# Moving the second MLP matrix to the end of a load stream, sharing nine slots, and writing the result in two halves

## The chip, the cores and the metric

The kernel runs on one core of a Trainium2 chip. The metric is the device time of one execution in microseconds (us). Before the change the median of the first three runs was 373.65 us. Ratios below are the mean time of one kernel's fast runs over the mean of the other kernel's fast runs of the same rounds on the same chip, so they are not quite the ratio of the medians quoted beside them.

Engines: PE multiplies matrices, PEld loads its stationary operand, DVE, ACT and POOL do elementwise work, and SP issues nearly all loads. A name such as SPq is an engine's instruction queue.

## The reference

A decode step for eight batch rows, in two branches that a gate mixes:

```python
x = A_x                                             # (8, 1, 576)
g = sigmoid((x * gate_w).sum(-1, keepdims=True))
q = x @ wq                                          # 32 heads of 128
k, v = the last 2048 rows of each of 16 K/V heads   # each serves 2 query heads
a = softmax(q k^T / sqrt(128)) v @ wo               # attention branch
b = gelu(layernorm(x) @ w1 + b1) @ w2 + b2          # MLP branch
return g * a + (1 - g) * b
```

All inputs are bf16. K and V are 134 MB of the 154 MB that are read; wq, wo, w1 and w2 are about 5 MB each. b2 has 576 elements.

## The kernel before

Every operation is recorded in a plan, a list scheduler on the host puts each engine's operations in an order, and that order is emitted. Each engine then executes its list in order and waits on semaphores. The scheduler has its own model of a load.

```python
class _Plan:
    DMA_BW = 428e3
    DMA_LAT = 1.8
    ...
    def schedule(self):
        ...
            if op.is_dma:
                eng_free[op.eng] = est + op.cost
                if op.nbytes < 65536:
                    op.t1 = est + 0.4 + self.DMA_LAT        # a small load: lands 2.2 us after its issue
                else:
                    start = max(est + 0.4, dma_free)        # a large one: behind those before it
                    dma_free = start + op.nbytes / self.DMA_BW
                    op.t1 = dma_free + self.DMA_LAT
```

The stream is made of units of 2 MB. A K unit is transposed by DVE and multiplied by PE, and four K units make the scores of one softmax group. A V unit is 64 small matmuls. Units are numbered from 0, so K31 and V31 are the last ones; the "last K pair" below is the two halves of K31. A unit's slot is free again when DVE (K) or PE (V) has used it. Before the change there are six slots, the output projection has 48 KB per partition of its own, W2 (`M` below) is loaded early, and V ends the stream:

```python
NSLOT = 6
stream = [("K", i) for i in range(4)] + [("M", i) for i in range(FC)]
stream += [("K", 4), ("W", 0), ("K", 5), ("W", 1), ("V", 0), ("W", 2), ("K", 6), ("W", 3)]
...                                              # then V and K in turn; V ends it
slot_free = [[o_qp], [o_qp], [o_qp], None, None, None]   # the first K waits for the query projection
```

Both branches add into one PSUM bank in `NJ` column groups that PE runs side by side. The bias is one such accumulation. Its load stands at the head, on ACT's queue:

```python
d_b2 = dma("act", lambda e: e.dma_start(b2_sb, B_b2.rearrange("(o d) -> o d", o=1)), "b", D * 2, name="d_b2", after=[d_b1])
...
o_m2 = [AccGroup("m2_b", [(ob[:, 0:8], b2_sb), (ob[:, 8:16], b2_sb)], db + [o_obl, o_obh], cost=0.6).op]
...
o_fin = add("dve", lambda e: e.tensor_copy(out_sb[0:104, :], ps[0:104, BK_ACC, 0:JN]), deps=acc_ops, name="fin", ...)
for j in range(NJ):                              # NJ = 4: two outputs on SP, two on ACT
    eng = "sp" if j % 2 == 0 else "act"
    fin.append(dma(eng, ... out2[:, JN * j:JN * j + JN], out_sb[32 * j:32 * j + 8, :] ...))
```

## Time and profile before

| what | number | where |
|---|---|---|
| time, span of the profiled run | 373.65 us, 372.1 us | runs, page |
| bytes read | 154.30 MB | DMA lines of the page |
| rate from 120 to 340 us | 430 GB/s at DMA share 1.01 | windows |
| a K load, issue to landing | 22.8 us | DMA issues of the page |
| first K issue | 24.71 us | timeline of SP |
| last landing to output issue | 368.04 to 369.76 us | timeline |

The table of forty slices on the page, lines for the DMA engines and for what they moved:

```profile
DMA  8999999999999999999999999999999999999992
GB/s 341 423 395 424 425 423 413 420 419 414 437 430 423 433 433 426 430 430 431 431 426 435 422 431 430 429 431 426 431 433 428 428 433 430 426 428 436 424 413 94
```

The DMA engines are busy from the first slice to the last, so only what keeps them idle or what stands before and after them can be saved. Three such places show. The first two are in the windows below. Columns are the stretch, its length, the busy time of each engine, the clock granted to PE, the share of the DMA engines that was busy, and the rate.

```profile
24.00:26.00 2.00, 1.48 (x30) 1.02 (x27) 0.42 (x1) 0.00 (x0) 0.00 (x0) 1.00 0.70 280
26.00:28.00 2.00, 0.27 (x3) 0.07 (x2) 0.00 (x0) 1.02 (x1) 0.53 (x3) 1.00 1.02 400
...
362.00:363.00 1.00, 0.70 (x26) 0.71 (x27) 0.00 (x0) 0.00 (x0) 0.00 (x0) 0.50 0.90 369
363.00:364.00 1.00, 1.00 (x44) 1.00 (x42) 0.00 (x0) 0.00 (x0) 0.00 (x0) 0.50 0.60 246
364.00:365.00 1.00, 0.80 (x31) 0.72 (x28) 0.00 (x0) 0.00 (x0) 0.00 (x0) 0.50 0.53 217
365.00:366.00 1.00, 0.38 (x15) 0.29 (x11) 0.00 (x0) 0.00 (x0) 0.00 (x0) 0.50 0.50 205
366.00:367.00 1.00, 0.59 (x16) 0.51 (x16) 0.00 (x0) 0.00 (x0) 0.00 (x0) 0.50 0.36 139
```

There is a small hole at 24 to 26 us, where the first K load waited for its slots, and a ramp at the end, where the share falls to about a half for some four microseconds. The packet records (the trace's list of every DMA packet with its start, duration and size) have 16 data packets in flight at 350 us and 8 at 365 us, so about half of the 16 DMA engines are done early. A window counts a whole packet where it starts. Spread over their durations, the packets put the hole at 26 to 28 us, with a share of 0.81, which is about 0.4 us of idle engines. The third place is the chain after the last landing, here from the timeline (start, duration, engine, line, operation):

```profile
368.05 0.59 PE L673 MATMUL ps<-arena 128*128 128x8 bf16 x16 [1.43 <-DMA arena<-in_A_v_cache_dram]
368.68 0.23 DVE L695 TENSOR_TENSOR arena<-ps,arena 128x16 bf16<-128x16 f32 x1 [13.64 <-PE ps L673]
368.96 0.41 PE L534 MATMUL ps<-arena 128*8 128x144 bf16 x8 [0.32 <-DVE arena L695]
369.42 0.31 DVE L729 CAST arena<-ps 104x144 bf16<-104x144 f32 x1 [0.52 <-PE ps L534]
369.76 0.75 SPq L733 DMA_DIRECT2D out_dram<-arena  x2
```

### The profile page before, as it was taken

How to read it: one execution, taken by the hardware profiler on the slowest of the kernel's cores; microseconds unless marked ns; L12 is line 12 of the kernel's file. 1: busy time of each engine (PE TensorE's matmuls, PEld its weight loads, DVE VectorE, ACT ScalarE, POOL GpSimd, SP SyncE). 2: the span in 40 equal slices, each digit the busy share in tenths (PEclk: the TensorE clock that was granted, in tenths of full speed). 3: DMA queues.
4: the chain of work that ended last, by engine and by line, in shares of the span. 5: the costliest groups of instructions: out<-in, count | busy, mean ns of one | idle time of the engine just before them, and what ended most of it. 6: DMA issues, size and time to landing. Idle time of an engine off the chain costs nothing.

```text
span 372.1 us, 7310 instructions
## 1 busy us (share of the span) xinstructions
PE 254.1 (68%) x3259; PEld 138.9 (37%) x3259; DVE 210.4 (57%) x253; ACT 28.3 (8%) x84; POOL 37.5 (10%) x163
## 2 busy tenths in 40 slices
PE   0169995661684987496749786877859774987554
PEld 0159432230341553243324443433415332543453
DVE  1414596934159645974468646954585448754600
ACT  1010001100002000200020001100020002000300
POOL 7003011010100110010100110011001010000000
PEclk9999999695865988788886868697659666788855
DMA  8999999999999999999999999999999999999992
GB/s 341 423 395 424 425 423 413 420 419 414 437 430 423 433 433 426 430 430 431 431 426 435 422 431 430 429 431 426 431 433 428 428 433 430 426 428 436 424 413 94
DMA packets 15097, 154.77 MB, mean 416 GB/s; under 512 B 1349, under 2 KB 5462, under 8 KB 6234
## 3 DMA queue, kind: packets, MB, share of 16 engines
q1 hardware_dynamic: 14992, 154.28, 97.9%
q8 instruction: 25, 0.41, 0.4%
q10 hardware_dynamic: 74, 0.03, 0.0%
q14 instruction: 6, 0.05, 0.0%
HBM read 154.30 MB, written 0.01 MB: 415 GB/s over the span
## 4 chain that ended last, share of the span: by engine, by line
DMA 50%; DVE 25%; PE 15%; SPq 8%; issue 1%; DVEq 0%
DMA arena<-in_A_k_cache_dram 37%; DVE arena L629 15%; PE ps L643 11%; DMA arena<-in_B_w_dram 7%; DMA arena<-in_A_v_cache_dram 6%; DVE arena L595 4%; DVE arena L576 4%; SPq L666 3%; SPq L719 2%; PE ps L491 2%; SPq L614 2%; DVE arena L585 1%; DVE arena L579 1%; PE ps L493 1%; PE ps L639 0%
## 5 line engine op out<-in xcount | busy, mean ns | idle before, releaser
L629 DVE STREAM_TRANSPOSE arena<-arena 128x2048 f32<-128x2048 f32 x64 | 145.6, 2298 | 85.8 <-DMA arena<-in_A_k_cache_dram 79.9
L643 PE MATMUL ps<-arena 128*128 128x512 bf16 x512 | 161.8, 476 | 39.0 <-DVE arena L629 39.0
L643 PEld LDWEIGHTS ps<-arena 128*128 128x128 bf16 x512 | 55.5, 115 | 133.5 <-issue 55.0
L673 PEld LDWEIGHTS ps<-arena 128*128 128x128 bf16 x2048 | 56.3, 97 | 13.7 <-DMA arena<-in_A_v_cache_dram 8.5
L673 PE MATMUL ps<-arena 128*128 128x8 bf16 x2048 | 56.7, 166 | 6.8 <-DMA arena<-in_A_v_cache_dram 6.8
L622 POOL COPY arena<-arena 32x32 bf16<-32x32 bf16 x128 | 26.0, 203 | 191.4 <-PE ps L643 175.5
L639 PE MATMUL ps<-arena 128*128 128x512 bf16 x32 | 14.9, 621 | 39.6 <-DVE arena L595 33.1
L576 DVE TENSOR_REDUCE arena<-ps 128x1 f32<-128x2048 f32 x8 | 18.3, 2292 | 27.1 <-PE ps L643 27.1
L590 ACT ACTIVATE arena<-ps,arena 128x512 bf16<-128x512 f32 x32 | 21.5, 685 | 111.2 <-DVE arena L585 111.2
L595 DVE STREAM_TRANSPOSE arena<-arena 128x512 bf16<-128x512 bf16 x32 | 19.9, 676 | 0.9 <-ACT arena L590 0.9
L639 PEld LDWEIGHTS ps<-arena 128*128 128x128 bf16 x32 | 3.5, 127 | 44.7 <-DVE arena L595 33.5
L689 ACT ACTIVATE arena<-ps 128x16 f32<-128x16 f32 x15 | 2.8, 184 | 182.2 <-PE ps L673 182.2
L695 POOL TENSOR_TENSOR arena<-arena 128x16 bf16<-128x16 f32 x15 | 4.0, 264 | 121.3 <-ACT arena L689 106.6
L534 PE MATMUL ps<-arena 128*8 128x144 bf16 (+1 forms) x280 | 8.4, 235 | 6.2 <-POOL arena L695 4.9
L491 PE MATMUL ps<-arena 128*128 128x8 bf16 x144 | 10.9, 201 | 1.7 <-DMA arena<-in_B_w_dram 1.7
L491 PEld LDWEIGHTS ps<-arena 128*128 128x128 bf16 x144 | 10.8, 157 | 2.2 <-DMA arena<-in_B_w_dram 2.2
L413 PE MATMUL ps<-arena 8*128 8x8 bf16 x8 | 0.5, 167 | 12.6 <-DVE arena L386 8.8
L534 PEld LDWEIGHTS ps<-arena 128*8 128x8 bf16 (+1 forms) x280 | 3.9, 84 | 11.3 <-POOL arena L695 5.7
L695 DVE TENSOR_TENSOR arena<-ps,arena 128x16 bf16<-128x16 f32 x1 | 0.2, 228 | 13.6 <-PE ps L673 13.6
L601 DVE RECIPROCAL arena<-ps 128x32 f32<-128x32 f32 x8 | 2.8, 353 | 7.9 <-PE ps L600 7.9
L493 PE MATMUL ps<-arena 128*128 128x8 bf16 x36 | 7.2, 201 | 0.0
L600 PEld LDWEIGHTS ps<-arena 128*128 128x128 f32 x16 | 4.2, 268 | 6.6 <-DVE arena L599 4.5
(78 smaller groups left out, 76.0 us busy)
## 6 DMA issues: line engine op xcount, KB each, us to landing
arena<-in_A_k_cache_dram SPq DMA_DIRECT2D x32, 2048.0 KB, 22.8
arena<-in_A_v_cache_dram SPq DMA_DIRECT2D x31, 2048.0 KB, 24.0
arena<-in_B_w_dram SPq DMA_DIRECT2D x4, 1296.0 KB, 16.1
arena<-in_B_w_dram SPq DMA_DIRECT2D x1, 4608.0 KB, 24.4
arena<-in_A_wo_dram SPq DMA_DIRECT2D x4, 1152.0 KB, 17.6
arena<-in_A_wq_dram SPq DMA_DIRECT2D x1, 4096.0 KB, 12.8
arena<-in_A_v_cache_dram SPq DMA_DIRECT2D x4, 512.0 KB, 21.9
arena<-in_B_w_dram SPq DMA_DIRECT2D x1, 576.0 KB, 25.6
```

Of the source, the lines that this page charges most:

```text
L491: ins = e.matmul(out_, lhsT, yT[:, kt, :], start=(kt == 0), stop=False)
L493: ins = e.matmul(out_, lhsT, yT[:, 4 + c // 2, :], start=False, stop=True)
L534: ins = e.matmul(ps[32 * j:32 * j + 8, BK_ACC, 0:JN], lhsT, rhs[:, JN * j:JN * j + JN], start=False, stop=True, skip_group_check=True, til ...
L576: mx = add("dve", lambda e: e.tensor_reduce(out=k(MX), in_=ps[:, 0:4, :].rearrange("p a n -> p (a n)"), axis=AXL.X, op=ALU.max), deps=[qk_ ...
L590: return e.activation(out=Pm[:, 512 * c:512 * c + 512], in_=ps[:, c, :], func=ACTF.Exp, bias=k(NB), scale=SCALE, accum_out=k(SUM + c))
L595: pts.append(add("dve", (lambda c=c: lambda e: e.transpose(PT[:, g % 2, 16 * c:16 * c + 16, :].rearrange("p r m -> p (r m)"), Pm[:, 512 * ...
L622: return e.tensor_copy(dst, src)
L629: tr = add("dve", (lambda h=h, kb=kb: lambda e: e.transpose(bass.AP(arena_f, offset=foffs("KT") + kb * 2048, ap=[[AST // 2, 128], [1, 2048]]),
L639: mm = e.matmul(ps[:, rc, :], maskL, maskR, start=True, stop=False)
L643: mm = e.matmul(ps[:, rc, :], qbd[:, ub, 2 * h + ee, :], rhs, start=False, stop=(q == 3 and h == 1 and ee == 1))
L666: d = dma("sp", (lambda pp=pp, w=w: lambda e: e.dma_start(slot(s)[:, pp * w:(pp + 1) * w], src[:, :, pp * w:(pp + 1) * w]))(), ("t%d" % pp ...
L673: mm = e.matmul(ps[:, BK_OS[item % 2], 8 * (q % 2):8 * (q % 2) + 8], slot(s)[:, r * 128:(r + 1) * 128], PT[:, g % 2, r, 8 * q:8 * q + 8], ...
```

## The change

Its intent is to shorten that last chain and to keep the stream fed. The projection weights no longer have memory of their own; they go through the slots, of which there are now nine. W2 ends the stream, because one W2 slice needs two matmuls before the result is complete, where V needs its products, the scaling and the projection. The result is accumulated in two column groups of 288 instead of four of 144, and evacuated by DVE and ACT at once, each with one write of its half. Two smaller moves come along: the small part of wq is loaded first, and b2 is broadcast to eight partitions and loaded on SP's queue just before W2.

```diff
-    NSLOT = 6
+    NSLOT = 9
-    NJ = 4
+    NJ = 2
-        req("wo", Hq * WOP, BF, 512)
...
-        d_b2 = dma("act", lambda e: e.dma_start(b2_sb, B_b2.rearrange("(o d) -> o d", o=1)), "b", D * 2, name="d_b2", after=[d_b1])
...
-        stream = [("K", i) for i in range(4)] + [("M", i) for i in range(FC)]
-        stream += [("K", 4), ("W", 0), ("K", 5), ("W", 1), ("V", 0), ("W", 2), ("K", 6), ("W", 3)]
+        stream = [("K", i) for i in range(5)]
...                      # K and V in turn; one W chunk after every eighth V
+        stream += [("B", 0)] + [("M", i) for i in range(FC)]
-        slot_free = [[o_qp], [o_qp], [o_qp], None, None, None]
+        slot_free = [[o_qp]] * 3 + [[o_hp]] * 3 + [[]] * 3
-            return (0, 1, 2, 0)[n] if n < 4 else (n - 3) % NSLOT
+            return (n + 6) % NSLOT
...
+        def bias(i):
+            d = dma("sp", lambda e: e.dma_start(b2_sb, B_b2.partition_broadcast(8)), "b2", 8 * D * 2, name="d_b2", after=last_dma[-1:])
+            last_dma.append(d)
+            o_m2.append(AccGroup("m2_b", [(ob[:, 0:8], b2_sb), (ob[:, 8:16], b2_sb)], [d, o_obl, o_obh], cost=0.6).op)
...                      # m2_chunk takes a slot; its last chunk is loaded in parts of 4, 3 and 2 slices
-        o_fin = add("dve", lambda e: e.tensor_copy(out_sb[0:104, :], ps[0:104, BK_ACC, 0:JN]), deps=acc_ops, name="fin", cost=0.3, prio=9)
+        for j, (eng, ev) in enumerate((("sp", "dve"), ("act", "act"))):
+            ...          # each engine evacuates one half of 288 columns, each queue writes one
```

More of the change, by code (lines that the diff above doesn't have):

```diff
@@ L183, in build_kernel @@
     NG = Hkv // HG
-    NSLOT = 6
+    NSLOT = 9
     SE = 4 * W
-    LEAD = 7
     FC, FJ = 4, 9
@@ L189, in build_kernel @@
     FCW = 128 * FJ
-    W2P = 5376
     WOP = 768
-    NJ = 4
+    NJ = 2
+    WO_CH = 8
     JN = D // NJ
@@ L245, in build_kernel @@
         req("o32", 2 * 16, F32)
-        req("oT", 2 * 16, BF)
+        req("oT", Hkv * 16, BF)
         req("out_sb", JN, BF)
@@ L294, in build_kernel @@
         b1T = view("b1T")
-        b2_sb = view("b2", 1)
+        b2_sb = view("b2", 8)
         u_sb, uh_sb, v1_sb, v2_sb = view("u"), view("uh"), view("v1"), view("v2")
         hT = view("hT").rearrange("p (t b) -> p t b", b=8)
-        ob = view("ob", 1)
-        ot32 = view("ot32", 1)
+        ob = view("ob", 8)
+        ot32 = view("ot32", 8)
         gb = view("gb")
@@ L305, in build_kernel @@
         o32 = view("o32").rearrange("p (u m) -> p u m", u=2)
-        oT = view("oT").rearrange("p (u h b) -> p u h b", u=2, h=2)
+        oT = view("oT").rearrange("p (u h b) -> p u h b", u=Hkv, h=2)
         out_sb = view("out_sb")
@@ L309, in build_kernel @@
         Pm = view("P")
-        wo_sb = view("wo").rearrange("p (t c) -> p t c", t=Hq)
         RAW = view("RAW")
@@ L325, in build_kernel @@
         w1_r = RAW[:, W1O + 4 * F:W1O + 4 * F + F // 2]
-        w2_sb = RAW[:, 3 * SE:3 * SE + FC * W2P].rearrange("p (c k) -> p c k", c=FC)
         def col(i, parts=128):
@@ L340, in build_kernel @@
         eng_sems = {e: es.enter_context(nc.semaphore("sem_" + e)) for e in ENGS}
-        dma_keys = ["x", "b", "wq", "w1", "wo", "out", "outb"] + ["w2_%d" % i for i in range(FC)] + ["s%d" % i for i in range(NSLOT)] + ["t%d" % i for i in range(4)]
+        dma_keys = ["x", "b", "b2", "wq", "w1", "out", "outb"] + ["s%d" % i for i in range(NSLOT)] + ["t%d" % i for i in range(4)]
         dma_sems = {k: es.enter_context(nc.semaphore("dma_" + k)) for k in dma_keys}
@@ L372, in build_kernel @@
         d_b1 = dma("act", lambda e: e.dma_start(b1c, B_b1.rearrange("(c f) -> c f", c=FC)), "b", F * 2, name="d_b1", after=[d_gw])
-        d_b2 = dma("act", lambda e: e.dma_start(b2_sb, B_b2.rearrange("(o d) -> o d", o=1)), "b", D * 2, name="d_b2", after=[d_b1])
         dx = [d_x, d_gw]
-        db = [d_b1, d_b2]
-        d_wqm = dma("sp", lambda e: e.dma_start(wq_m.rearrange("p t c -> p (t c)"), A_wq[0:512, :].rearrange("(p t) c -> p (t c)", t=4)), "wq", 512 * 8192, name="d_wqm")
-        d_wqr = dma("sp", lambda e: e.dma_start(wq_r, A_wq[512:576, :].rearrange("k (s c) -> (k s) c", s=2)), "wq", 64 * 8192, name="d_wqr", after=[d_wqm])
+        db = [d_b1]
+        d_wqr = dma("sp", lambda e: e.dma_start(wq_r, A_wq[512:576, :].rearrange("k (s c) -> (k s) c", s=2)), "wq", 64 * 8192, name="d_wqr")
+        d_wqm = dma("sp", lambda e: e.dma_start(wq_m.rearrange("p t c -> p (t c)"), A_wq[0:512, :].rearrange("(p t) c -> p (t c)", t=4)), "wq", 512 * 8192, name="d_wqm", after=[d_wqr])
         dwq = [d_wqm, d_wqr]
-        d_w1m = dma("sp", lambda e: e.dma_start(w1_m.rearrange("p t c -> p (t c)"), B_w1[0:512, :].rearrange("(p t) c -> p (t c)", t=4)), "w1", 512 * F * 2, name="d_w1m", after=[d_wqr])
+        d_w1m = dma("sp", lambda e: e.dma_start(w1_m.rearrange("p t c -> p (t c)"), B_w1[0:512, :].rearrange("(p t) c -> p (t c)", t=4)), "w1", 512 * F * 2, name="d_w1m", after=[d_wqm])
         d_w1r = dma("sp", lambda e: e.dma_start(w1_r, B_w1[512:576, :].rearrange("k (s c) -> (k s) c", s=2)), "w1", 64 * F * 2, name="d_w1r", after=[d_w1m])
@@ L441, in build_kernel @@
         o_gb = add("dve", lambda e: e.tensor_copy(gb, ps[:, BK_X, 384:400]), deps=[o_gp], name="gb_ev", cost=0.15)
-        o_obh = add("dve", lambda e: e.tensor_copy(ob[:, 0:8], gb[0:1, 8:16]), deps=[o_gb], name="ob_hi", cost=0.12)
+        o_obh = add("dve", lambda e: e.tensor_copy(ob[:, 0:8], dg[:, 8:16]), deps=[o_dgb], name="ob_hi", cost=0.12)
         o_ob32 = add("dve", lambda e: e.tensor_copy(ot32, ob[:, 0:8]), deps=[o_obh], name="ob_32", cost=0.12)
-        o_obl = add("dve", lambda e: e.tensor_tensor(out=ob[:, 8:16], in0=gb[0:1, 8:16], in1=ot32, op=ALU.subtract), deps=[o_ob32], name="ob_lo", cost=0.12)
+        o_obl = add("dve", lambda e: e.tensor_tensor(out=ob[:, 8:16], in0=dg[:, 8:16], in1=ot32, op=ALU.subtract), deps=[o_ob32], name="ob_lo", cost=0.12)
         o_i32 = []
@@ L541, in build_kernel @@
         NUQ = 4 * NG
-        stream = [("K", i) for i in range(4)] + [("M", i) for i in range(FC)]
-        stream += [("K", 4), ("W", 0), ("K", 5), ("W", 1), ("V", 0), ("W", 2), ("K", 6), ("W", 3)]
-        ki, vi = 7, 1
+        stream = [("K", i) for i in range(5)]
+        ki, vi = 5, 0
         while ki < NUQ or vi < NUQ:
-            if vi < NUQ:
-                stream.append(("V", vi)); vi += 1
             if ki < NUQ:
-                stream.append(("K", ki)); ki += 1
-        WO_CH = 8
-        d_woc = []
+                stream.append(("K", ki))
+                ki += 1
+            if ki >= 6:
+                stream.append(("V", vi))
+                if (vi + 1) % (NUQ // (Hq // WO_CH)) == 0:
+                    stream.append(("W", vi // (NUQ // (Hq // WO_CH))))
+                vi += 1
+        stream += [("B", 0)] + [("M", i) for i in range(FC)]
         last_dma = [d_w1r]
-        slot_free = [[o_qp], [o_qp], [o_qp], None, None, None]
+        slot_free = [[o_qp]] * 3 + [[o_hp]] * 3 + [[]] * 3
         n_slot = [0]
@@ L658, in v_unit, with pv_fn @@
             item = 2 * g + q // 2
-            final = (i == NUQ - 1)
-            src = src_of(A_v_cache, g, q)
-            parts = 4 if final else 1
-            prev = None
-            for pp in range(parts):
-                nr = 64 // parts
-                w = nr * 128
-                d = dma("sp", (lambda pp=pp, w=w: lambda e: e.dma_start(slot(s)[:, pp * w:(pp + 1) * w], src[:, :, pp * w:(pp + 1) * w]))(),
-                        ("t%d" % pp) if final else ("s%d" % s), 4 * W * Dh * 2 // parts, deps=slot_free[s] if pp == 0 else [], name="dv%d_%d" % (i, pp), after=last_dma[-1:])
-                last_dma.append(d)
-                def pv_fn(e, pp=pp, nr=nr):
-                    mm = None
-                    for r in range(pp * nr, (pp + 1) * nr):
-                        mm = e.matmul(ps[:, BK_OS[item % 2], 8 * (q % 2):8 * (q % 2) + 8], slot(s)[:, r * 128:(r + 1) * 128], PT[:, g % 2, r, 8 * q:8 * q + 8],
-                                      start=(q % 2 == 0 and r == 0), stop=(r == 63), skip_group_check=True)
-                    return mm
-                deps = [d] + pt_done[g]
-                if q % 2 == 0:
-                    deps += [o_item_ev[item - 2]] if item >= 2 else [o_qT, o_u]
-                prev = add("pe", pv_fn, deps=deps, name="pv%d_%d" % (i, pp), cost=2.2 / parts, after=[prev] + pv_hist[-1:])
+            d = dma("sp", lambda e: e.dma_start(slot(s), src_of(A_v_cache, g, q)), "s%d" % s, 4 * W * Dh * 2, deps=slot_free[s], name="dv%d" % i, after=last_dma[-1:])
+            last_dma.append(d)
+            def pv_fn(e):
+                mm = None
+                for r in range(64):
+                    mm = e.matmul(ps[:, BK_OS[item % 2], 8 * (q % 2):8 * (q % 2) + 8], slot(s)[:, r * 128:(r + 1) * 128], PT[:, g % 2, r, 8 * q:8 * q + 8],
+                                  start=(q % 2 == 0 and r == 0), stop=(r == 63), skip_group_check=True)
+                return mm
+            deps = [d] + pt_done[g]
+            if q % 2 == 0:
+                deps += [o_item_ev[item - 2]] if item >= 2 else [o_qT, o_u]
+            prev = add("pe", pv_fn, deps=deps, name="pv%d" % i, cost=2.2, after=pv_hist[-1:])
             pv_hist.append(prev)
@@ L686, in v_unit @@
                 hl = q // 2
-                pj = [proj_ops[item - 2]] if item >= 2 else []
                 if item < Hkv - 1:
@@ L690, in v_unit @@
                     o_item_ev[item] = ev
-                    eng, src_, deps = "pool", o32[:, item % 2, :], [ev, rg_done[g]] + pj
+                    eng, src_, deps = "pool", o32[:, item % 2, :], [ev, rg_done[g]]
                 else:
-                    eng, src_, deps = "dve", ps[:, bk, 0:16], [prev, rg_done[g]] + pj
+                    eng, src_, deps = "dve", ps[:, bk, 0:16], [prev, rg_done[g]]
                 def om_fn(e):
-                    return e.tensor_tensor(out=oT[:, item % 2, :, :].rearrange("p h b -> p b h"), in0=src_.rearrange("p (b h) -> p b h", h=2),
+                    return e.tensor_tensor(out=oT[:, item, :, :].rearrange("p h b -> p b h"), in0=src_.rearrange("p (b h) -> p b h", h=2),
@@ L696, in om_fn @@
                                            in1=rg[:, g % 2, 16 * hl:16 * hl + 16].rearrange("p (b h) -> p b h", h=2), op=ALU.mult)
                 oT_done[item] = add(eng, om_fn, deps=deps, name="oT%d" % item, cost=0.25, prio=9)
-                mms = [(oT[:, item % 2, h, :], wo_sb[:, 2 * item + h, 0:D]) for h in range(2)]
-                proj_ops[item] = AccGroup("proj%d" % item, mms, [oT_done[item]] + d_woc, cost=0.6, after=[g_.op for g_ in acc_groups[-1:]], prio=2).op
-        o_m2 = [AccGroup("m2_b", [(ob[:, 0:8], b2_sb), (ob[:, 8:16], b2_sb)], db + [o_obl, o_obh], cost=0.6).op]
@@ L703, in m2_chunk, with wo_chunk @@
-        def m2_chunk(ci):
-            d = dma("sp", lambda e: e.dma_start(w2_sb[:, ci, 0:FJ * D], B_w2[FCW * ci:FCW * ci + FCW, :].rearrange("(p j) n -> p (j n)", j=FJ)),
-                    "w2_%d" % ci, FCW * D * 2, deps=[o_hp], name="d_w2_%d" % ci, after=last_dma[-1:])
-            last_dma.append(d)
-            mms = [(hT[:, FJ * ci + j, :], w2_sb[:, ci, j * D:(j + 1) * D]) for j in range(FJ)]
-            o = AccGroup("m2_%d" % ci, mms, [o_hT, d], cost=2.5, after=o_m2[-1:]).op
-            o_m2.append(o)
-            for s in range(3, 6):
-                slot_free[s] = [o]
+        def wo_chunk(i):
+            s = take_slot()
+            h0 = WO_CH * i
+            dst = slot(s)[:, 0:WO_CH * WOP].rearrange("p (t c) -> p t c", t=WO_CH)
+            d = dma("sp", lambda e: e.dma_start(dst[:, :, 0:D], A_wo[128 * h0:128 * (h0 + WO_CH), :].rearrange("(t p) c -> p t c", p=128)),
+                    "s%d" % s, WO_CH * 128 * D * 2, deps=slot_free[s], name="d_wo%d" % i, after=last_dma[-1:])
+            last_dma.append(d)
+            ops = []
+            for item in range(h0 // 2, (h0 + WO_CH) // 2):
+                mms = [(oT[:, item, h, :], dst[:, 2 * item + h - h0, 0:D]) for h in range(2)]
+                ops.append(AccGroup("proj%d" % item, mms, [oT_done[item], d], cost=0.5).op)
+            slot_free[s] = ops
@@ new lines, in build_kernel @@
+        o_m2 = []
+        def bias(i):
+            d = dma("sp", lambda e: e.dma_start(b2_sb, B_b2.partition_broadcast(8)), "b2", 8 * D * 2, name="d_b2", after=last_dma[-1:])
+            last_dma.append(d)
+            o_m2.append(AccGroup("m2_b", [(ob[:, 0:8], b2_sb), (ob[:, 8:16], b2_sb)], [d, o_obl, o_obh], cost=0.6).op)
+        def m2_chunk(ci):
+            s = take_slot()
+            dst = slot(s)[:, 0:FJ * D]
+            src = B_w2[FCW * ci:FCW * ci + FCW, :].rearrange("(p j) n -> p (j n)", j=FJ)
+            cuts = [0, 4, 7, 9] if ci == FC - 1 else [0, FJ]
+            ops = []
+            for n, (j0, j1) in enumerate(zip(cuts, cuts[1:])):
+                d = dma("sp", (lambda j0=j0, j1=j1: lambda e: e.dma_start(dst[:, j0 * D:j1 * D], src[:, j0 * D:j1 * D]))(),
+                        ("t%d" % n) if ci == FC - 1 else ("s%d" % s), 128 * (j1 - j0) * D * 2, deps=slot_free[s] if n == 0 else [], name="d_w2_%d_%d" % (ci, n), after=last_dma[-1:])
+                last_dma.append(d)
+                mms = [(hT[:, FJ * ci + j, :], dst[:, j * D:(j + 1) * D]) for j in range(j0, j1)]
+                ops.append(AccGroup("m2_%d_%d" % (ci, n), mms, [o_hT, d], cost=0.25 * (j1 - j0), after=o_m2[-1:]).op)
+                o_m2.append(ops[-1])
+            slot_free[s] = ops
@@ L713, in build_kernel @@
         pv_hist = []
         for kind, i in stream:
-            if kind == "M":
-                m2_chunk(i)
-            elif kind == "W":
-                h0 = WO_CH * i
-                d = dma("sp", (lambda h0=h0: lambda e: e.dma_start(wo_sb[:, h0:h0 + WO_CH, 0:D], A_wo[128 * h0:128 * (h0 + WO_CH), :].rearrange("(t p) c -> p t c", p=128)))(),
-                        "wo", WO_CH * 128 * D * 2, name="d_wo%d" % i, after=last_dma[-1:])
-                last_dma.append(d)
-                d_woc.append(d)
-            elif kind == "K":
-                k_unit(i)
-            else:
-                v_unit(i)
+            {"K": k_unit, "V": v_unit, "W": wo_chunk, "M": m2_chunk, "B": bias}[kind](i)
@@ L728, in build_kernel, with ev_fn @@
         acc_ops = [g_.op for g_ in acc_groups]
-        o_fin = add("dve", lambda e: e.tensor_copy(out_sb[0:104, :], ps[0:104, BK_ACC, 0:JN]), deps=acc_ops, name="fin", cost=0.3, prio=9)
         fin = []
-        for j in range(NJ):
-            eng = "sp" if j % 2 == 0 else "act"
-            fin.append(dma(eng, (lambda j=j: lambda e: e.dma_start(out2[:, JN * j:JN * j + JN], out_sb[32 * j:32 * j + 8, :]))(), "out" if j % 2 == 0 else "outb", 8 * JN * 2, deps=[o_fin], name="d_out%d" % j, after=last_dma[-1:]))
+        for j, (eng, ev) in enumerate((("sp", "dve"), ("act", "act"))):
+            def ev_fn(e, j=j, ev=ev):
+                dst, src = out_sb[32 * j:32 * j + 8, :], ps[32 * j:32 * j + 8, BK_ACC, 0:JN]
+                if ev == "dve":
+                    return e.tensor_copy(dst, src)
+                return e.activation(out=dst, in_=src, func=ACTF.Copy)
+            o_fin = add(ev, ev_fn, deps=acc_ops, name="fin%d" % j, cost=0.4, prio=9)
+            fin.append(dma(eng, (lambda j=j: lambda e: e.dma_start(out2[:, JN * j:JN * j + JN], out_sb[32 * j:32 * j + 8, :]))(), "out" if j == 0 else "outb", 8 * JN * 2, deps=[o_fin], name="d_out%d" % j, after=last_dma[-1:]))
```

## The prediction

> What bounds it now. The kernel is a stream of loads. By the page's DMA lines it reads 154.30 MB; the table of forty slices shows DMA digit 9 almost throughout, and ten-microsecond windows between 120 and 340 us hold 424 to 436 GB/s at a DMA share of 1.00 to 1.02. The Trainium skill ("DMA: Bandwidth & Descriptors", "Where 436 GB/s comes from") puts the port ceiling at 435 GB/s and also says HBM loads bind at about 358; this trace agrees with the first and not the second. So the middle has 1% at most left, and SP's waits for slots there (157 us for the transposes, 90 for the V products, by the table of waits) are not lost time: loads take 23 us from issue to landing, so almost five are queued while SP waits. At 429 GB/s the bytes need 359.7 of the 372.1 us. The other 12 us are the start, the small-packet stretch, and the end.
>
> The change removes no bytes (b2 now goes to eight partitions, 8 KB more). Costed:
>
> 1. Early hole. SP issues the first K load at 24.71 us, after the query projection frees its slots; windows show 280 GB/s at 24 to 26 us (share 0.70), 400 at 26 to 28. By the packet records the engines lose about 0.4 us there, and the next stretch runs at 393 to 410 GB/s. With slots 6 to 8 free from the start, K is issued at about 3 us. Gain 0.4 to 1.0 us.
>
> 2. Output projection. Its 4096 packets of 1152 B take 51 ns each against 614 ns for 16 KB, about 2 us more in all than their bytes need (60 to 90 us: 409 to 414 GB/s). Only their place moves. SP was held up to 6.9 us at issues behind them; nine slots keep enough queued. Zero.
>
> 3. Ramp at the end. From 362.5 us half of the DMA engines have finished and the rest go on to 366.9: windows of 1 us fall from 369 to 246, 217, 205, 139, 0 GB/s. That costs 2.1 us. It is a spread between engines that builds up over the stream; the change does not address it. Zero, plus or minus 1.
>
> 4. Chain after the last landing (368.04 us by the timeline). Before: 16 products 0.60, DVE 0.24, projection 0.41, DVE 0.31, with waits 1.72 us to the output issue at 369.76; then two issues a queue, 0.75 us. After: two hT slices by two column halves, four matmuls of 288 columns, at the half clock seen there (0.50) about 0.6 us; then halves of 288 columns on DVE and ACT in parallel, about 0.45 (144 columns took 0.31; ACT's 512 took 0.68); one issue a queue, 0.37. Saves 0.5 and 0.4: 0.9 us.
>
> All of 1 and 4 lies on the critical path. The larger PE time of the accumulations (8.4 us becomes perhaps 12) does not: PE is busy 68% and waits. The last K now lands about 12 us earlier before the end (W2's bytes), so V products and projections finish under the W2 loads.
>
> Sum: 0.6 + 0.9 and a little = 1.6 us. Predicted 372.0 us, 80% range 370.2 to 373.5. Chances: faster by over 2%: 0.02; within 2%: 0.97; slower: 0.01.
>
> Right if: no dip at 24 to 28 us and first K issue near 3 us; middle rate unchanged at 429; landing to output issue near 1.2 us, one output issue per queue. Step 2 is wrong if the DMA share falls under 1.00 in the middle behind the 1152 B packets.
>
> What would make it wrong: the spread between engines growing or vanishing; the scheduler placing a projection so that PE stalls on a late load and slots come free late; W2's short last packets slower than V's.

## The result and the profile after

The kernel became slower: 386.15 us (384.64 to 387.64, 4 runs) against 373.6 us, ratio 1.0337 with a 95% interval of 1.0291 to 1.0383. The prediction was 372.0 us with a range of 370.2 to 373.5, so it was wrong, in size and in direction.

The same two lines of the page, of the kernel after (its span is 385.9 us, so a slice is 9.6 us):

```profile
DMA  8999999999999999999999999999999999999430
GB/s 343 451 401 426 431 429 427 433 428 428 431 426 433 419 428 433 426 433 431 425 431 416 430 427 430 428 433 430 433 428 417 430 430 428 433 422 390 166 155 1
```

Up to about 356 us the stream is as full as before. After that the DMA engines run dry and then stand idle for a slice. The group table of the page names a wait that the kernel before did not have, in the line of the accumulations (after the bars: busy time, mean ns, idle time just before them and what ended it):

```profile
L529 PE MATMUL ps<-arena 128*8 128x288 bf16 (+1 forms) x140 | 11.5, 326 | 32.4 <-DMA arena<-in_B_b_dram 32.4
```

PE stood 32.4 us, all of it in one piece, for a load of a bias. The timeline shows where. SP's and PE's lines of it:

```profile
316.86 0.53 SPq L704 DMA_DIRECT2D arena<-in_B_b_dram  x1
319.84 1.74 PE L662 MATMUL ps<-arena 128*128 128x8 bf16 x64
321.61 43.49 SPq L715 DMA_DIRECT2D arena<-in_B_w_dram  x6
353.94 0.64 PE L529 MATMUL ps<-arena 8*8 8x288 bf16 x4 [32.36 <-DMA arena<-in_B_b_dram]
354.51 6.08 PE L640 MATMUL ps<-arena 128*128 128x512 bf16 x16
360.44 3.34 PE L662 MATMUL ps<-arena 128*128 128x8 bf16 x128
368.67 0.64 PE L597 MATMUL ps<-arena 128*128 128x32 f32 x2 [4.89 <-DVE arena L596]
369.12 7.00 PE L662 MATMUL ps<-arena 128*128 128x8 bf16 x256
376.05 7.43 PE L529 MATMUL ps<-arena 128*8 128x288 bf16 x88
383.62 0.45 DVE L733 CAST arena<-ps 8x288 bf16<-8x288 f32 x1 [7.24 <-PE ps L529]
384.10 0.32 SPq L736 DMA_DIRECT2D out_dram<-arena  x1
```

The chain of waits has the same load as its longest piece:

```profile
316.86 37.03 DMA arena<-in_B_b_dram
```

The four bias matmuls (8x288) were reached at 321.6 us. Their load, 9 KB, had been issued at 316.86 us and was there 37.0 us later. By the packet records 14.7 MB of loads issued before it were still to be moved at that moment, which is 34 us at 430 GB/s (an estimate). Behind them in PE's list stood everything that was left: the last K pair's products, the last softmax, six V units, the projections and W2. When the bias was in, that chain took another 30 us to the output issue, and the loads had gone dry meanwhile, because slots come free only when PE has used them. This is SP's table of waits between 361 and 363 us:

```profile
SPq L715 <- PE ps L662: 14.0, 1, 14.0
```

SP could issue the third W2 chunk only at 362.2 us, after V products that were late. The windows show both sides, an idle PE under a full stream, and then an idle stream under a busy PE:

```profile
330.00:340.00 10.00, 0.00 (x0) 0.00 (x0) 0.00 (x0) 0.00 (x0) 0.00 (x0) 0.50 1.00 429
340.00:350.00 10.00, 0.00 (x0) 0.00 (x0) 0.00 (x0) 0.00 (x0) 0.00 (x0) 0.50 1.01 420
350.00:356.00 6.00, 2.06 (x8) 0.65 (x9) 0.00 (x0) 0.00 (x0) 0.00 (x0) 0.50 0.97 397
356.00:364.00 8.00, 7.78 (x141) 4.78 (x139) 3.10 (x8) 0.00 (x0) 0.00 (x0) 0.79 0.30 102
```

Why do the bias matmuls stand there? The scheduler's plan answers it. These are the planned times (start and end in its own model), beside which the chip's times are 353.9 us for the landing and 353.94 us for the matmuls:

```
SP:  d_wo3 313.0-350.2   d_b2 313.4-315.6   d_w2_0_0 317.3-353.3
PE:  pv25 315.0-317.2   m2_b 317.2-317.8   qk31_0 320.5-322.5   qk31_1 322.8-324.8   pv26 324.8-327.0
```

The load before b2 was planned to land at 350.2 us and the one behind it at 353.3 us, but b2 itself at 315.6 us, because it is smaller than 64 KB and such loads are modelled as landing 2.2 us after their issue. That shortcut did no harm while the small loads stood at the head on ACT's queue. The Trainium skill says how both queues really behave. "DMA: Bandwidth & Descriptors", section "Queues, rings and completion order", has SP and ACT each own one ring on each of the 16 DMA engines, with descriptors consumed in ring order. So a small load on SP's queue comes behind the megabytes issued before it on that queue. "TensorE: Matmul & The Clock Gate", section "Step-by-step: what each phase is for", says that matmuls stay in program order and that only weight loads are pulled ahead. This trace agrees with both: 37.0 us for 9 KB, and 32.4 us in which no matmul passed the waiting one.

### The profile page after: what moved, and what is told of

It is laid out like the page before. It is cut to its first block, busy times and chain, and to the rows that moved or that the text cites. A ratio compares the mean times of both kernels' runs of the same rounds, so it can differ in the third digit from the quotient of the medians.

```text
span 385.9 us, 7069 instructions
## 1 busy us (share of the span) xinstructions
PE 248.2 (64%) x3117; PEld 138.3 (36%) x3117; DVE 210.4 (55%) x253; ACT 28.6 (7%) x85; POOL 37.8 (10%) x163
## 4 chain that ended last, share of the span: by engine, by line
DMA 62%; PE 22%; DVE 14%; issue 1%; SPq 1%; ACT 0%; DVEq 0%; ACTq 0%
DMA arena<-in_A_k_cache_dram 46%; PE ps L640 12%; DMA arena<-in_B_b_dram 10%; DVE arena L626 9%; DMA arena<-in_B_w_dram 7%; PE ps L662 3%; DVE arena L573 3%; PE ps L486 2%; PE ps L529 2%; PE ps L636 1%; DVE arena L592 1%; DVE arena L576 1%; PE ps L488 1%; DVE arena L582 0%; SPq L656 0%
## 5 line engine op out<-in xcount | busy, mean ns | idle before, releaser
L640 PE MATMUL ps<-arena 128*128 128x512 bf16 x512 | 153.9, 458 | 35.0 <-DVE arena L626 35.0
L640 PEld LDWEIGHTS ps<-arena 128*128 128x128 bf16 x512 | 53.7, 111 | 125.0 <-issue 45.7
L662 PEld LDWEIGHTS ps<-arena 128*128 128x128 bf16 x2048 | 55.9, 97 | 11.5 <-DMA arena<-in_A_v_cache_dram 6.8
L662 PE MATMUL ps<-arena 128*128 128x8 bf16 x2048 | 55.8, 166 | 5.0 <-DMA arena<-in_A_v_cache_dram 5.0
L636 PE MATMUL ps<-arena 128*128 128x512 bf16 x32 | 14.9, 620 | 37.8 <-DVE arena L592 29.3
L529 PE MATMUL ps<-arena 128*8 128x288 bf16 (+1 forms) x140 | 11.5, 326 | 32.4 <-DMA arena<-in_B_b_dram 32.4
L529 PEld LDWEIGHTS ps<-arena 128*8 128x8 bf16 (+1 forms) x140 | 6.5, 96 | 37.0 <-DMA arena<-in_B_b_dram 32.5
L636 PEld LDWEIGHTS ps<-arena 128*128 128x128 bf16 x32 | 3.5, 127 | 43.1 <-DVE arena L592 38.7
L486 PE MATMUL ps<-arena 128*128 128x8 bf16 x144 | 10.9, 201 | 6.9 <-DMA arena<-in_B_w_dram 6.9
L486 PEld LDWEIGHTS ps<-arena 128*128 128x128 bf16 x144 | 10.8, 157 | 7.4 <-DMA arena<-in_B_w_dram 7.4
L488 PE MATMUL ps<-arena 128*128 128x8 bf16 x36 | 7.2, 201 | 0.0
L587 ACT ACTIVATION_READ_ACCUMULATOR arena<-ps,arena 128x1 f32 x32 | 6.5, 203 | 0.0
```

Of the source, the lines that this page charges most:

```text
L486: ins = e.matmul(out_, lhsT, yT[:, kt, :], start=(kt == 0), stop=False)
L488: ins = e.matmul(out_, lhsT, yT[:, 4 + c // 2, :], start=False, stop=True)
L529: ins = e.matmul(ps[32 * j:32 * j + 8, BK_ACC, 0:JN], lhsT, rhs[:, JN * j:JN * j + JN], start=False, stop=True, skip_group_check=True, til ...
L587: return e.activation(out=Pm[:, 512 * c:512 * c + 512], in_=ps[:, c, :], func=ACTF.Exp, bias=k(NB), scale=SCALE, accum_out=k(SUM + c))
L636: mm = e.matmul(ps[:, rc, :], maskL, maskR, start=True, stop=False)
L640: mm = e.matmul(ps[:, rc, :], qbd[:, ub, 2 * h + ee, :], rhs, start=False, stop=(q == 3 and h == 1 and ee == 1))
```

## The experiments

Theory A is the one just given. The rivals were B, that the nine slots and SP's long stays at issues behind the small packets of wo (20 to 26 us) make loads late, and C, that two column groups double the PE time of the accumulations and that this is the long end. Letters in the expectations refer to these; rival D, which came later, is in the expectation of e5.

### e1_plan_b2_queued: tell the plan that b2 queues

Only the size that the plan is told is changed. A comparison of the two programs shows that four matmuls moved on PE, and that every other engine's list, SP's among them, is the same.

```diff
-            d = dma("sp", ... "b2", 8 * D * 2, name="d_b2", after=last_dma[-1:])
+            d = dma("sp", ... "b2", 65536, name="d_b2", after=last_dma[-1:])
```

> Edit: the schedule alone is told that the b2 load queues like a large one, so the four bias matmuls move on PE from before the last K pair to the end; every other instruction and every DMA stays where it was. Theory A (PE, which runs in order, stood 32.4 us at the bias matmuls for the b2 load that was queued behind the other loads): the stall vanishes, about 371.5 us (369.5 to 373.5), DMA share 1.0 up to about 362 us. Rival B (nine slots, SP held 20 to 26 us at issues behind the small packets, loads late): nothing changes, about 386. Rival C (two column groups double the PE time of the accumulations, 7.4 us at the end): about 386, at best 383.

Measured: 371.19 us (6 runs), ratio to before 0.9934 (0.9919 to 0.9949). The two lines of e1's PE where the stall was (timeline):

```profile
319.31 1.74 PE L662 MATMUL ps<-arena 128*128 128x8 bf16 x64
324.12 5.37 PE L640 MATMUL ps<-arena 128*128 128x512 bf16 x16 [3.07 <-DVE arena L626]
```

The last K pair is multiplied at 324.1 us, where in the kernel after it was at 354.5 us. SP was still held at the first W2 issue, in this trace too, and it cost nothing:

```profile
321.08 29.13 SPq L715 DMA_DIRECT2D arena<-in_B_w_dram  x6
```

So the place of four matmuls is worth 15 us, the whole loss and more. B and C are out as causes of it, since nine slots, the waits at issues and the two groups are all still there.

### e2_b2_at_head: load b2 early

```diff
+        d_b2 = dma("act", lambda e: e.dma_start(b2_sb, B_b2.partition_broadcast(8)), "b2", 8 * D * 2, name="d_b2", after=[d_b1])
...
-            d = dma("sp", lambda e: e.dma_start(b2_sb, B_b2.partition_broadcast(8)), "b2", ...)
```

> Edit: b2 is loaded at the head on ACT's queue, as in the kernel before, still to eight partitions; everything else as in the kernel after. Theory A: the same as e1 within 0.5 us, about 371.5 us. Rivals B and C: about 386.

Measured: 371.81 us (6 runs), ratio 0.9938 (0.9922 to 0.9955), the same as e1 within the intervals. With the load at the head, the plan also puts the four matmuls near the start of PE's list. Either repair will do: the matmuls behind the landing, or the landing before the matmuls.

### e7_b2_act_late: the same moment, another queue

Here PE's order is that of the slow kernel, and the load is still issued late, but by ACT.

```diff
-            d = dma("sp", lambda e: e.dma_start(b2_sb, B_b2.partition_broadcast(8)), "b2", 8 * D * 2, name="d_b2", after=last_dma[-1:])
-            last_dma.append(d)
+            d = dma("act", lambda e: e.dma_start(b2_sb, B_b2.partition_broadcast(8)), "b2", 8 * D * 2, name="d_b2", after=last_dma[-1:])
```

> Edit: the kernel after with the b2 load issued from ACT's queue instead of SP's, after ACT's evacuation of the item before (near 300 us), PE's order untouched: the bias matmuls still stand before the last K pair. Theory A in its narrow form (b2 was late because it stood in the same queue behind the large loads): on ACT's queue nothing stands before it, it lands within some us, PE is not held, 371 to 372 us. If instead every load of that moment is late because the DMA engines hold a backlog of 35 us whatever the queue: b2 lands 25 us or more after its issue, and the kernel stays at 376 us or more.

Measured: 371.66 us (6 runs), ratio 0.9945 (0.9929 to 0.9961). The timeline of ACT's queue and PE:

```profile
300.95 0.28 ACTq L704 DMA_DIRECT2D arena<-in_B_b_dram  x1
...
321.86 0.41 PE L529 MATMUL ps<-arena 8*8 8x288 bf16 x4
324.12 1.98 PE L640 MATMUL ps<-arena 128*128 128x512 bf16 x8 [1.85 <-DVE arena L626]
```

By the packet records of this trace the eight data packets of b2 began between 304.30 and 305.02 us, and the last semaphore packet at 305.48 us, which is 4.5 us after the issue. SP's loads in that trace still took 34 us from issue to landing. The backlog therefore belongs to the queue and not to the engines as such, and a load on the other queue slips in between. ACT issued it 16 us earlier than SP had, so this is not the same instant, but 4.5 us against 37.0 us does not depend on that. The narrow form of theory A stands.

### e3_before_b2_late and e5_before_b2_last: the same mistake in the kernel before

If the late bias is enough by itself, it must hurt the old kernel too. Both runs move its b2 load to SP's queue, e3 between V26 and V27 and e5 behind V29, and let the plan place the matmuls.

```diff
-        d_b2 = dma("act", ... name="d_b2", after=[d_b1])
+        def bias():
+            d = dma("sp", lambda e: e.dma_start(b2_sb, B_b2.rearrange("(o d) -> o d", o=1)), "b2", D * 2, name="d_b2", after=last_dma[-1:])
+            last_dma.append(d)
+            AccGroup("m2_b", [(ob[:, 0:8], b2_sb), (ob[:, 8:16], b2_sb)], [d, o_obl, o_obh], cost=0.6)
...
+            if (kind, i) == ("V", NUQ - 5):      # e5: NUQ - 2
+                bias()
```

> Edit in the kernel BEFORE: its b2 load moves from the head to SP's queue between the loads of V26 and V27, and its bias matmuls follow where the schedule puts them (before the last K pairs); six slots, four column groups, V last all stay. Theory A: PE stands about 20 us at the bias matmuls (the loads of this kernel take 22 to 24 us to land), slots come free late, and the kernel becomes 5 to 14 us slower than before, 379 to 387 us. Rivals B and C: 373.6, unchanged, since nothing of what they blame is in it.

Measured for e3: 374.12 us (4 runs), ratio 1.0013 (0.9989 to 1.0036). This was a miss; the stall is there but is nearly free. Its line in the timeline:

```profile
338.89 0.41 PE L533 MATMUL ps<-arena 1*8 1x144 bf16 x8 [11.40 <-DMA arena<-in_B_b_dram]
```

The load was 18.6 us on its way (issued at 320.31 us), and PE had other work for part of that, so it stood 11.4 us and not 20. The stall ended 35 us before the end, and PE, busy about two thirds of the time, caught up while the queued loads arrived: the DMA share stayed at 0.97 to 1.03 from 340 to 360 us. What I had left out is that a stall must be longer or later than this slack.

> Edit in the kernel BEFORE, as in e3, but the b2 load stands behind V29 on SP's queue, and the bias matmuls before the products of the last K pair. In e3 the stall was only 11.4 us and ended 35 us before the end, and the loads in flight covered it. Theory A (a late stall of PE costs what is left of the chain behind it once the queued loads no longer cover it): b2 lands near 358 us, PE stands about 20 us until then, and the chain behind it (K products 5.4, maximum and exponentials 8, V products 7, projection and output 3) ends near 381 us, so 379 to 385 us. Rival D (the stall costs only when it keeps the DMA queue from being fed, which it does not here, since all loads are issued): 374 us.

Measured for e5: 381.78 us (4 runs), ratio 1.0209 (1.0194 to 1.0224), which is clearly slower, though not clearly by over 2%. The time is as theory A said, although b2 landed at 352.6 us and not near 358, and PE stood 14.35 us and not 20:

```profile
352.56 0.75 PE L533 MATMUL ps<-arena 1*8 1x144 bf16 x16 [14.35 <-DMA arena<-in_B_b_dram]
```

The stall is only 3 us longer than in e3 but ends 14 us later, and costs about 8 us. The DMA windows of e5 show a share of 1.00 from 350 to 360 us and 0.41 from 360 to 370 us, with all loads issued by 344.6 us, so here the stream was never starved. What costs is the serial work left behind the stall; rival D is out. In the kernel after both happen, that chain and, from 356 to 364 us, a starved stream.

### e6_after_six_slots: the fault with a shallower queue

```diff
-    NSLOT = 9
+    NSLOT = 6
```

> Edit: the kernel after with six slots instead of nine; the b2 load stays in its place in the stream and is still planned as landing at once. With six slots it is issued later, and the schedule now puts the bias behind the last K products. Theory A: the stall then holds up only the last four V products and the projections, 372 to 375 us. If the other parts of the change (stream order, column groups, output halves) were to blame: 385.

Measured: 375.17 us (4 runs), ratio 1.0037 (1.0022 to 1.0053), just above the expected 372 to 375 us. With six slots b2 is issued at 332.21 us and not at 316.86 us, the plan puts the bias behind the last K products, and it holds up only the last V products:

```profile
354.67 0.64 PE L529 MATMUL ps<-arena 8*8 8x288 bf16 x4 [20.70 <-DMA arena<-in_B_b_dram]
```

So rival B had part of the truth: nine slots are not slow, but they let the load be issued, and planned, so early that the bias came before K31, and they made the queue in front of it 37 us long, where it was 22.5 us with six.

### e4_four_column_groups: the output part of the kernel after undone

The edit takes the four groups, the single evacuation and the four outputs of the kernel before into the kernel after, stall included.

```diff
-    NJ = 2
+    NJ = 4
-        for j, (eng, ev) in enumerate((("sp", "dve"), ("act", "act"))): ...
+        o_fin = add("dve", lambda e: e.tensor_copy(out_sb[0:104, :], ps[0:104, BK_ACC, 0:JN]), deps=acc_ops, name="fin", cost=0.3, prio=9)
```

> Edit: the kernel after with four column groups of 144, one evacuation on DVE and four outputs as before; the bias stays where it is. Theory A: the stall is still there; only the catch-up at the end is shorter, 382 to 386 us. Rival C: about 373. Rival B: about 386.

Measured: 384.62 us (4 runs), ratio 1.029 (1.0269 to 1.031), with PE waiting 32.8 us for b2. That is 1.5 us less than the kernel after by the medians, but the intervals overlap (1.0291 to 1.0383 for the kernel after). So the output part with its two groups is at most a small part of the loss, and so is rival C.

### f1, f2, f3, f5, f6: what the parts are worth without the stall

These take one part of the change back in e1 (f5 in e2) and test whether my costing of the rest was right.

f1_fixed_four_groups is e1 with the output edit of e4.

> Edit: e1 (bias planned where it belongs) with the old output part: four column groups of 144, one evacuation on DVE, two outputs a queue. My costing of the output part: the two extra issues cost 0.4 us, but the last matmuls and the evacuation are shorter (four groups at once), so 0.1 to 0.5 us slower than e1, 371.3 to 371.8. Rival: the two column groups made PE late at the end (it ran 4.5 us without a gap in e1), then f1 is as fast as e1 or faster, 370.5 to 371.2.

f2_fixed_old_head is e1 with wq's large part first again, and with the first three K units in the slots that wait for the query projection:

```diff
-            return (n + 6) % NSLOT
+            return (0, 1, 2, 6, 7, 8, 3, 4, 5)[n % NSLOT]
```

> Edit: e1 with the old head: the large part of the query weights loads first, and the first three K loads take the slots that the query projection must free. My costing: the hole at 24 to 28 us is back and costs 0.4 to 1.0 us, so 371.6 to 372.2. If the head is worth nothing, 371.2.

f3_fixed_six_slots is e1 with `NSLOT = 6`.

> Edit: e1 (bias planned as queued) with six slots instead of nine. My costing gave the extra slots nothing beyond the early hole (at most 0.4 to 1.0 us), since the DMA share was 1.00 with six: 371.2 to 372.2. Rival: depth itself pays (fewer idle moments of the engines in the middle): 373 or more. And beside e6 (six slots, bias planned as landing at once, 375.2 us) it tells what the stall still cost there: 3 to 4 us.

f5_v_last is e2 with this order, the last V in four parts as before, and the last four projections behind it:

```diff
+        stream = stream[:-2] + [("W", 3), ("B", 0)] + [("M", i) for i in range(FC)] + [("V", NUQ - 1)]
```

> Edit: e2 (b2 at the head, no stall) with the last V load, in four parts as before, behind W2 instead of before it; nine slots, two column groups and the two output halves stay. My costing of the chain behind the last landing: V last adds the 16 products, the scaling on DVE and a wait, in place of two W2 slices that cost about as much as the projection, 0.5 to 1.0 us: 371.9 to 372.8. Rival: the order of the last loads is worth nothing, 371.2 to 371.8 as e1 and e2.

f6_quarters is e1 with four groups whose quarters DVE and ACT copy to the same eight partitions, so that one output a queue is left:

```diff
+                    dst, src = out_sb[0:8, JN * j:JN * j + JN], ps[32 * j:32 * j + 8, BK_ACC, 0:JN]
```

> Edit: e1 with four column groups of 144 (PE half as long on the last slices), evacuated by DVE and ACT in two copies each to the same eight partitions, so that one output a queue remains. If f1 was slow for its second outputs alone and the four groups were good: 370.6 to 371.1, that is up to 0.4 us faster than e1. If the four groups themselves cost: 371.5 or more.

| kernel | median us | ratio to before (95%) | against its base |
|---|---|---|---|
| e1, base of f1, f2, f3, f6 | 371.19 | 0.9934 (0.9919 to 0.9949) | |
| e2, base of f5 | 371.81 | 0.9938 (0.9922 to 0.9955) | |
| f1 old output part | 372.63 | 0.9972 (0.9960 to 0.9985) | +1.4 us |
| f2 old head | 371.94 | 0.9951 (0.9939 to 0.9964) | +0.6 us |
| f3 six slots | 372.29 | 0.9960 (0.9943 to 0.9977) | +1.0 us |
| f5 V last | 372.24 | 0.9958 (0.9945 to 0.9972) | +0.7 us |
| f6 quarters | 372.37 | 0.9964 (0.9950 to 0.9978) | +1.1 us |

The last column is the difference of the ratios times 373.7 us. Most of the intervals overlap with that of the base, and f1, f2, f3 and f5 add up to 3.7 us where the whole is worth 2.5 us (1 minus 0.9934, times 373.7 us), so these sizes are rough. Only f1 and, barely, f6 are clear of e1 by their intervals. f1 missed its expectation in both forms: 372.63 us lies above the 371.8 us that the two extra outputs were to explain. f6, which has no second outputs, was expected at 370.6 to 371.1 us if the groups were good and at 371.5 us or more if the groups themselves cost, and it is 372.37 us.

The traces do not put that cost on the groups. These are the last steps of f6 (timeline):

```profile
367.60 0.41 PE L529 MATMUL ps<-arena 128*8 128x144 bf16 x8 [0.18 <-DMA arena<-in_B_w_dram]
368.86 0.32 SPq L738 DMA_DIRECT2D out_dram<-arena  x1
```

And this is e1's last load, the last part of W2 (DMA issues: KB, us from issue to landing):

```profile
arena<-in_B_w_dram SPq DMA_DIRECT2D x1, 288.0 KB, 16.6
```

It was issued at 349.78 us and landed at 366.4 us, but PE was still busy with earlier W2 products, and the four matmuls that needed it began only at 367.1 us. From the landing to the first output issue e1 took 1.9 us. In f6 PE waited for the load, and the same stretch took 1.3 us (f1: 0.9 us). So two groups put some 0.6 us of PE work behind the last landing. But the last load of f6 and f1 landed at 367.6 us, 1.1 us later than in e1. There, from about 366.3 us on, the packets of the last load went one after another. A late end also shows in the profiled run of e2 (367.3 us), which has two groups, so it isn't shown that the groups cause it, and why f1 and f6 are slower than e1 stays open.

f2 came out in its range but does not prove the cause I gave: its hole did not come back, since its first K load went out at 20.54 us, while the w1 loads still ran, and its window from 24 to 26 us reads 393 GB/s at a share of 0.95, like e1's 381 GB/s at 0.95. f3 bears on the slots as a whole; at 372.29 us it is just above its range of 371.2 to 372.2 and below the rival's 373. Its fixed plan costs 2.9 us less than e6's (0.9960 against 1.0037), a little less than the 3 to 4 us expected.

The last steps of e1 in the timeline, which answer to those of before:

```profile
363.32 4.49 PE L529 MATMUL ps<-arena 128*8 128x288 bf16 x36 [0.78 <-DMA arena<-in_B_w_dram]
367.93 0.40 ACT L734 ACTIVATE arena<-ps 8x288 bf16<-8x288 f32 x1 [24.60 <-PE ps L529]
367.94 0.45 DVE L733 CAST arena<-ps 8x288 bf16<-8x288 f32 x1 [14.78 <-PE ps L529]
368.42 0.32 SPq L736 DMA_DIRECT2D out_dram<-arena  x1
```

And its windows at the end, the ramp:

```profile
362.00:363.00 1.00, 0.54 (x6) 0.00 (x0) 0.00 (x0) 0.00 (x0) 0.00 (x0) 0.50 0.62 253
363.00:364.00 1.00, 0.68 (x8) 0.37 (x9) 0.00 (x0) 0.00 (x0) 0.00 (x0) 0.50 0.53 220
364.00:365.00 1.00, 1.00 (x12) 0.58 (x10) 0.00 (x0) 0.00 (x0) 0.00 (x0) 0.50 0.52 211
365.00:366.00 1.00, 1.00 (x12) 0.58 (x10) 0.00 (x0) 0.00 (x0) 0.00 (x0) 0.50 0.44 173
```

e1 is 0.7% faster than the kernel before and 15 us faster than the kernel after, and is the version to keep; e2 and e7 are the same within the intervals.

## Why the prediction was wrong

The step that failed is this one: "The last K now lands about 12 us earlier before the end (W2's bytes), so V products and projections finish under the W2 loads." It holds only if PE is free to work when the last K lands. I had costed the move of b2 as bytes alone ("b2 now goes to eight partitions, 8 KB more") and did not ask when those bytes would land and which engine would stand in front of what until then. The runs showed 37.0 us from issue to landing, 32.4 us of standing for PE, and a cost of 15 us (386.15 against 371.19 us in e1). The prediction did list "the scheduler placing a projection so that PE stalls on a late load and slots come free late" among what could make it wrong. That is the mechanism, with the bias in the place of a projection, but it was given almost no chance (0.01 for slower), although both facts were there to be read: the diff moves a load to a queue whose loads take 23 us to land, and the scheduler's code calls a small load landed 2.2 us after its issue.

Point by point, with e1 as the change without that fault:

1. The early hole: right in kind. The first K load was issued at 2.63 us, and the stretch from 26 to 28 us went from 400 to 432 GB/s. By the packet records 16.07 MB had been moved by 40 us, against 15.76 MB before, which is about 0.7 us at 429 GB/s (an estimate). No run isolates this worth, since f2 took the head back without bringing the hole back.
2. The projection's small packets: right. From 120 to 340 us the kernel after kept 428 GB/s at a share of 1.01, although SP stood up to 26 us at an issue.
3. The ramp: right. e1 still goes from 253 to 173 GB/s over its last four full windows, about as before.
4. The chain after the last landing: right in sum, but not in its parts. By the packet records the last data packet ended at 366.97 us before and 366.04 us in e1, the outputs were issued at 369.76 and 368.36 us, and the spans ended at 372.1 and 370.2 us. That is 2.8 and 2.3 us before, 2.3 and 1.8 us in e1, so 1.0 us saved against 0.9 predicted. But the prediction counted from the landing and forecast about 1.2 us to the output issue. It took 1.7 us before and 1.9 us in e1, because the two groups kept PE busy past the landing (the 4.49 us without a gap above). So the claim that the larger PE time of the accumulations is not on the critical path failed too, by some 0.6 us. The sum came right because the landing followed the last data packet after 0.4 us in e1 and after 1.0 us before. Nothing had forecast that, so this part is luck.

With the fault removed the predicted 372.0 us is met by 371.19 us, inside the range: in the profiled runs the last data packet ended 0.9 us earlier and the chain behind it was 1.0 us shorter. That the sum agrees doesn't prove each term, since the end of the loads alone differs by about 1 us between the profiled runs of e1, e2, f1 and f6. What decided the result was the term that was missing from the sum.

## What to carry to other kernels

When a load moves to another queue or another place in a stream, cost its landing, not its bytes: on a full queue it lands behind what was issued before it, here 37 us for 9 KB, while the other queue delivered it in 4.5 us. Where an engine's order comes from a planner, check that the planner models small loads as queued too, because an in-order engine holds everything behind a wait, and deeper buffering can make such an error larger (PE stood 20.7 us with six slots, 32.4 us with nine). A stall costs little while loads are queued and its end is far from the kernel's end (11.4 us for almost nothing in e3), and much near the end (14.35 us of standing cost 8 us in e5).

## What the Trainium skill lacked or had wrong

- "DMA: Bandwidth & Descriptors", "Where 436 GB/s comes from": it says that loads from HBM are bound at about 358 GB/s a core, and does not say there that this is with both cores of the HBM domain loading, as a note in the page's section "Bandwidth" does. With this one core running, the traces hold 428 to 430 GB/s from 120 to 340 us, near its other figure, the port ceiling of 435 GB/s.
- The same page, "Anatomy of one DMA", puts the fixed part of a DMA at about 2 us, for a DMA that GpSimd issues. The page has no figure for a small load on a busy queue of SP or ACT. Behind a full stream on SP's queue 9 KB took 37.0 us, and 4.5 us on ACT's. The order of the rings is on the page, but not this consequence with a number.
- The same page, "Latency and other measured facts", calls DMA engines 7 and 15 usually slower, with a guess about loads that GpSimd issues. It has nothing on half of the engines finishing late. Here the DMA share falls to 0.50 to 0.60 for three microseconds at the end of the kernel before, with 8 data packets in flight at 365 us. The packet records do not name the engine, so which they are and why is open.
